# The same instructions on other SBUF addresses: new homes for the operands of TensorE

## The chip, the cores and the metric

The kernel runs on one NeuronCore of a Trainium2 chip. The metric is the device time of one execution in microseconds (us), the median of three runs. An address in this document is a byte offset within a partition of SBUF; "home" is the address at which a tile begins, and its remainder in 256 is what the change sets.

## The reference

Pooled attention, and then two products with a rational function between them:

```python
k_p = k.reshape(B, H, S // 8, 8, D).mean(axis=3)          # v_p the same
attn = softmax(q @ k_p.T / sqrt(D))                       # B = H = 8, S = 576, D = 64
x = (attn @ v_p).transpose(0, 2, 1, 3).reshape(4608, 512)
h = x @ w_in                                              # 512 x 2048
g = (a0 + a1*h + a2*h*h + a3*h**3) / (1 + |b0|*|h| + |b1|*h*h + 1e-6)
out = g @ w_out                                           # 2048 x 512
```

All inputs and the output are float32.

## The kernel before

The 4608 tokens are worked on in 18 blocks of 256, and the 2048 hidden columns in 8 units of 256. Every large operand is split into two parts, a rounded one and what is left of it (`x` into `xs[0]`, `xs[1]`; `w_in` into `win0` to `win7`; `w_out` into `wout0` to `wout7`; the rational's result into `gh`, `gl`), and a product is three passes over such parts. The parts are of the type float32r.

For block i and unit u, `mm1` makes `ph`: six groups of four matmuls. In each matmul a slice of 128x128 of `win{u}` is the stationary operand, which a LDWEIGHTS brings into the array, and 128x256 of x is the moving operand, which streams through. `rational` then makes `gh` and `gl` on ScalarE, VectorE and GpSimd, and `mm2` makes `po`: six groups of two matmuls, where 128x128 of `gh` or `gl` is stationary and 128x512 of `wout{u}` moves. The attention of a block (`ps`, `pm`, `pv` and so on) stands between such groups.

The order on every engine comes from a planner (`Plan.solve`), which lists all operations with estimated costs and due times and simulates the five engines; `Plan.issue` then issues them in that order. `mm2` of a unit is due four units after its `mm1` (`LAG`), so that TensorE goes back and forth: four matmuls of `mm1` of one unit, two of `mm2` of the unit four before, four of `mm1`, and so on. Such a piece of four and two is called a group here. In a steady stretch unit 1's groups hold products with `wout5`, unit 2's with `wout6` (the first still with `wout5`), and so on around. There are 18 x 8 x 6 = 864 pieces of each kind.

Tiles get their addresses from pools. A pool lays its tiles one behind the other in the order of their first use, in steps of 32 bytes, and the pools lie behind each other in the order in which they are opened. In the kernel before, all sixteen weight tiles stand in `cpool` together with small constants and the attention's tiles, `x` stands in `work2` behind the small tiles `mx` and `sm`, and `gh` and `gl` in `work3`. Every slice that a matmul reads begins a multiple of 256 bytes behind its tile's home (512 within `win`, 1024 within `x`, 2048 within `wout`, 512 or 1024 within `gh` and `gl`), and the buffers of a ring lie 2048 or 4096 bytes apart; so the remainder in 256 of a home holds for every slice of it.

Of the kernel before, what the change touches and what calls it, by code (L numbers as in the profile page):

```python
# [8 lines left out]
F32 = mybir.dt.float32  # L9
F32R = mybir.dt.float32r  # L10
# [62 lines left out]
class Buf:  # L73
# [7 lines left out]
    def real(self):  # L81
        if self.it is None:
            self.it = self.ring.pool.tile(self.shape, self.dtype, tag=self.ring.tag,
                                          name=self.name)
        return self.it
# [233 lines left out]
def tile_pooled_attention_then_rational_moe(  # L319
# [20 lines left out]
    P = 128  # L340
    G = 8
    SP = S // G
    NJ = H // 2
    REM = 2 * SP - P
    RW = G * D
    TOK = 256
# [10 lines left out]
    pools = {}  # L357

    def pool(name, bufs, loose=False, **kw):
        pools[name] = ctx.enter_context(tc.tile_pool(name=name, bufs=bufs, **kw)), bufs, loose  # L360

    pool("cpool", 1)
    pool("stage", 2)
    pool("work1", 1)
    pool("work2", 2)
    pool("dec", 2, loose=True)
    pool("rat", 5)
    pool("work3", 3)
    pool("ps", 8, loose=True, space=PS)
    pool("hbm", 1, space=bass.MemoryType.DRAM)  # L370

    def new(where, tag, shape, dtype, name):
        return plan.tile(*pools[where], shape, dtype, tag, name)

    def bank(name, shape):
        return new("ps", "ps", shape, F32, name)
# [5 lines left out]
    def pe(ns, calls, claims=(), after=()):  # L382
        return plan.add("pe", ns / 1000, calls, claims=claims, after=after)

    def mm(out, lhsT, rhs, start, stop):
        return "matmul", (out,), dict(lhsT=lhsT, rhs=rhs, start=start, stop=stop)

    def dma(kbytes, dst, src, run=2048, issue=0.48, early=60.0, after=()):

        plan.add("sp", issue, [("dma_start", (dst, src), {})], early=early, after=after,  # L390
                 bytes=kbytes * 1024 * (1 + 312 / run))
# [4 lines left out]
    real = pools["cpool"][0].tile  # L396
    ones = pools["dec"][0].tile([P, P], F32, tag="m", name="ones")
    identr = real([P, P], F32R, tag="identr", name="identr")
    ident = identr.bitcast(F32)
    zero = real([P, 1], F32R, tag="zero", name="zero")  # L400
    masks = new("cpool", "masks", [P, 6], F32, "masks")

    spread = new("work1", "vs", [P, 3 * P], F32, "fourfold")
# [4 lines left out]

    mrem_lo, mrem = ([masks[:, i + m:i + m + 1] for m in range(2)] for i in (2, 4))
    QC = 1.0 + 1e-6  # L410
    cbias = real([P, 1], F32, tag="cbias", name="cbias")

    def small(name, *args, **kw):
        plan.add("pool", 0.13, [(name, args, kw)])
# [30 lines left out]
    CW = 2 * DM  # L445
# [20 lines left out]
    spare = [["win7", "wout7", "wout6", "win6"], ["win5", "wout5", "wout4"]]  # L466
    held = {}

    def early(n, at):
        if (n, at) not in held:  # L470
            held[n, at] = new("cpool", spare[n][at], [P, 2 * CW], F32, f"early{n}_{at}")
        return held[n, at]

    w_in32, w_out32 = w_in.bitcast(I32), w_out.bitcast(I32)
# [1 line left out]

    def load_weights(kind, u):
        name = f"{kind}{u}"
        raw = new("cpool", name, [P, 2 * CW], F32, "r" + name)
        if kind == "win":  # L480
            dma(1024, raw.bitcast(I32).rearrange("p (k x) -> p k x", x=4 * P),
                w_in32[:, u * 4 * P:(u + 1) * 4 * P].rearrange("(k p) x -> p k x", p=P))
        else:
            dma(1024, raw.bitcast(I32).rearrange("p (f x) -> p f x", f=2),
                w_out32[u * 2 * P:(u + 1) * 2 * P, :].rearrange("(f p) x -> p f x", p=P), run=4096)
        words = raw.bitcast(I32).rearrange("p (n t) -> p n t", t=2)
        hw, lw = words[:, :, 1], words[:, :, 0]
        m = new("dec", "m", [P, CW], F32, f"m_{name}")
        mi = m.bitcast(I32)
        act(CW + 100).activation(m, hw.bitcast(F32), AF.Prelu, scale=2.0 ** -111, alpha=-2.0 ** 32)  # L490
        dve(CW, port=True, rate=0.52).tensor_scalar(
            out=mi, in0=mi, scalar1=3, scalar2=None, op0=ALU.logical_shift_left)
        dve(CW, port=True).scalar_tensor_tensor(
            out=mi, in0=lw, scalar=29, in1=mi, op0=ALU.logical_shift_right, op1=ALU.bitwise_or)
        w = new("cpool", name, [P, 2, CW], F32R, name)
        act(CW).copy(w[:, 0, :], m)
        gp(CW).tensor_tensor(out=w[:, 1, :], in0=m, in1=w[:, 0, :].bitcast(F32),
                             op=ALU.subtract)
        weights[kind, u] = w
# [165 lines left out]
    def segs(t0, n):  # L665

        r, t = [], t0
        while t < t0 + n:
            e = min(t0 + n, (t // S + 1) * S)
            r.append((t - t0, e - t0, t // S))  # L670
            t = e
        return r
# [148 lines left out]

    def values(i, hi, lo, before=None):

        xs = [new("work2", f"x{s}", [P, NJ, TOK], F32R, f"x{s}_{i}") for s in range(2)]
        for c in range(2):
            if before:
                before(c)
            pv = bank(f"pv{i}_{c}", [P, 2, TOK])
            calls = []
            for jj in range(2):  # L830
                j = 2 * c + jj
                for r0, r1, n in segs(i * TOK, TOK):
                    vh, vl = vm[n % 2]
                    o = pv[:, jj, r0:r1]
                    terms = ((o, vh[:, j, :], hi[:, j, r0:r1]), (o, vl[:, j, :], hi[:, j, r0:r1]),
                             (pv[:D, jj, r0:r1], vr[n % 2][:, j, :], lo[:, NJ + c, r0:r1]),
                             (o, vh[:, j, :], lo[:, j, r0:r1]))
                    calls += [mm(dst, vals, probs, s == 0, s == 3)
                              for s, (dst, vals, probs) in enumerate(terms)]
            pe(117.4 * 8 if len(calls) == 8 else 1635, calls, claims=xs)  # L840
            cs = slice(2 * c, 2 * c + 2)
            act(2 * TOK).copy(xs[0][:, cs, :], pv)
            dve(2 * TOK).tensor_tensor(
                out=xs[1][:, cs, :], in0=pv, in1=xs[0][:, cs, :].bitcast(F32),
                op=ALU.subtract)
        return xs
# [9 lines left out]
    def attend(i):  # L856
# [27 lines left out]
        if i >= SQ:  # L884

            for a in range(4):
# [15 lines left out]
            dve(2 * TOK, port=True).tensor_tensor(  # L902
                out=both[0], in0=both[1], in1=own, op=ALU.subtract)
        return values(i, hi, lo)


# [6 lines left out]
        return kept  # L913

    def reload(i, kept):
        xs = [new("work2", f"x{s}", [P, NJ, TOK], F32R, f"xr{s}_{i}") for s in range(2)]
        for x, d in zip(xs, kept):
            dma(512, x.bitcast(F32), d, run=4096)
        return xs
# [19 lines left out]

    def rational(i, u, ph):  # L940
        t, w, r = (new("rat", "rat", [P, 2, TOK], F32, f"{x}{i}_{u}") for x in "twr")
        gh = new("work3", "gh", [P, 2, TOK], F32R, f"gh{i}_{u}")
        gl = new("work3", "gl", [P, 2, TOK], F32R, f"gl{i}_{u}")
        rp = bank(f"rp{i}_{u}", [P, 2, TOK])

        n = 2 if last(i, u) else 1
        for k in range(n):
            f = slice(k, k + 1) if n == 2 else slice(0, 2)
            quotient(2 * TOK // n, *(x[:, f, :] for x in (ph, t, w, r, rp, gh, gl)),
                     (t, w, r), (gl,))  # L950
        return gh, gl

    def last(i, u):
        return i == NBLK - 1 and u == NU - 1

    def quotient(W, h, t, w, r, rp, gh, gl, early, late):
        act(W, claims=early).activation(w, h, AF.Abs, scale=1.0 / WS)
        act(W + 200).activation(t, h, AF.Identity, bias=na2, scale=na3)
        act(W + 260).activation(r, w, AF.Identity, bias=b0, scale=b1)
        gp(W).tensor_tensor(out=w, in0=w, in1=r, op=ALU.mult)  # L960
        dve(W).tensor_tensor(out=t, in0=t, in1=h, op=ALU.mult)
        dve(W + 50).scalar_tensor_tensor(
            out=t, in0=t, scalar=na1, in1=h, op0=ALU.add, op1=ALU.mult)
        act(W + 30).activation(rp, w, AF.Ln, bias=QC)
        act(W + 10).activation(rp, rp, AF.Exp, scale=-1.0)
        dve(W + 50).scalar_tensor_tensor(
            out=t, in0=t, scalar=na0, in1=rp, op0=ALU.add, op1=ALU.mult)
        dve(W).scalar_tensor_tensor(
            out=rp, in0=w, scalar=QC, in1=rp, op0=ALU.add, op1=ALU.mult)
        dve(W).scalar_tensor_tensor(  # L970
            out=t, in0=rp, scalar=-2.0, in1=t, op0=ALU.add, op1=ALU.mult)
        act(W, claims=late).copy(gh, t)
        gp(W).tensor_tensor(out=gl, in0=t, in1=gh.bitcast(F32), op=ALU.subtract)
# [73 lines left out]
    xs, kept = {}, {}  # L1047
    for at, (i, u) in enumerate(order):
# [19 lines left out]
        gh, gl = rational(i, u, ph)  # L1068
# [44 lines left out]
```

## Time and profile before

| | |
|---|---|
| median of 3 runs | 940.96 us (940.87 to 941.06) |
| profiled execution, first to last instruction | 940.1 us |
| TensorE matmul busy | 929.1 us, 99% |
| TensorE weight load busy | 845.3 us, 90% |
| VectorE, ScalarE, GpSimd busy | 763.6, 677.6, 530.8 us |
| `ph` matmuls, `po` matmuls | 3456 and 1728 |

The profile gives a span, from the first instruction to the last, and no other time of that execution; the 0.9 us between the span and the median lie around it. A matmul's busy time overlaps that of the next one, so what a matmul costs is read from the start of one to the start of the next, and not from its mean duration.

### The profile page before, as it was taken

Reading aid. Unit: us, or ns where it says so; the run is one execution under the profiler, and the core shown is the slowest. Engines: PE = TensorE matmul, PEld = TensorE weight load, DVE = VectorE, ACT = ScalarE, POOL = GpSimd, SP = SyncE. Lnnn points to the kernel's source line nnn. Section 1 sums busy time; section 2 is a strip of 40 time slices with the busy share of each in tenths; the row PEclk is TensorE's granted clock in tenths of the full one; section 3 lists DMA queues with packets and bytes.
Section 4 is the critical chain, followed back from the end, with each engine's and each line's share of the span. In section 5 each row is a group of like instructions: output and inputs, shape, how many; then the busy total and the mean of one; then the engine's idle time right before and its main releaser. Section 6 shows DMA issues by size and latency. Waiting matters only on the chain.

```text
span 940.1 us, 17117 instructions
## 1 busy us (share of the span) xinstructions
PE 929.1 (99%) x6158; PEld 845.3 (90%) x6158; DVE 763.6 (81%) x1335; ACT 677.6 (72%) x1126; POOL 530.8 (56%) x474
## 2 busy tenths in 40 slices
PE   7999999999999999999999999999999999999998
PEld 7899999989999999999999899999999899999996
DVE  6889987688879777878888788878886988787764
ACT  3788888667677767776776867686867786777764
POOL 5776788685447544445644574457543754444452
PEclk9999999999999999999999999999999999999999
DMA  9995201163233412122603160215212231202000
GB/s 282 306 378 176 46 29 46 40 161 87 47 79 76 115 24 58 26 59 51 141 9 70 41 155 10 39 41 129 69 27 53 68 80 23 57 1 58 1 23 23
DMA packets 185072, 75.32 MB, mean 80 GB/s; under 512 B 162332, under 2 KB 162332, under 8 KB 184988
## 3 DMA queue, kind: packets, MB, share of 16 engines
q1 hardware_dynamic: 184988, 74.23, 30.9%
q8 instruction: 49, 0.80, 0.4%
q14 instruction: 35, 0.29, 0.1%
HBM read 50.59 MB, written 12.58 MB: 67 GB/s over the span
## 4 chain that ended last, share of the span: by engine, by line
PE 95%; DMA 3%; SPq 2%; issue 0%; ACT 0%
PE po L299 43%; PE ph L299 43%; PE pv L299 4%; PE ps L299 4%; SPq L299 2%; DMA early<-in_v_dram 1%; DMA q<-in_q_dram 1%; PE pvs L299 1%; PE pk L299 0%; PE pvr L299 0%; PE pq L299 0%; PE pm L299 0%; PE po L290 0%; PE pr L299 0%; PE pl L299 0%
## 5 line engine op out<-in xcount | busy, mean ns | idle before, releaser
L299 PEld LDWEIGHTS ph<-x,win 128*128 128x128 f32 x3264 | 484.4, 188 | 61.7 <-DVE x L299 0.5
L299 PE MATMUL ph<-x,win 128*128 128x256 f32 x3264 | 507.5, 282 | 0.5 <-DVE x L299 0.3
L299 PE MATMUL po<-wout,gh 128*128 128x512 f32 x1152 | 356.9, 396 | 0.0
L299 POOL TENSOR_TENSOR w<-w,r 128x512 f32<-128x512 f32 (+1 forms) x145 | 193.8, 1336 | 269.9 <-ACT r L299 268.2
L299 POOL TENSOR_TENSOR gl<-t,gh 128x512 fp32r<-128x512 f32 (+1 forms) x145 | 190.8, 1316 | 79.5 <-ACT gh L299 78.2
L299 PEld LDWEIGHTS po<-wout,gh 128*128 128x128 f32 x1152 | 182.3, 189 | 7.8 <-issue 0.4
L299 PE MATMUL po<-wout,gl 128*128 128x512 f32 x576 | 181.7, 396 | 0.0
L299 DVE SCALAR_TENSOR_TENSOR t<-t,abn,rp 128x512 f32<-128x512 f32 (+1 forms) x145 | 106.9, 738 | 51.8 <-ACT rp L299 50.0
L299 ACT ACTIVATE t<-ph,abn 128x512 f32<-128x512 f32 (+1 forms) x145 | 112.2, 774 | 40.7 <-PE ph L299 30.2
L299 DVE TENSOR_TENSOR t<-t,ph 128x512 f32<-128x512 f32 (+1 forms) x145 | 97.8, 676 | 41.9 <-ACT t L299 41.0
L299 ACT ACTIVATE r<-w,abn 128x512 f32<-128x512 f32 (+1 forms) x145 | 117.7, 812 | 13.3 <-POOL gl L299 6.6
L299 ACT ACTIVATE w<-ph 128x512 f32<-128x512 f32 (+1 forms) x145 | 86.1, 594 | 54.8 <-PE ph L299 34.8
L299 ACT ACTIVATE rp<-w 128x512 f32<-128x512 f32 (+1 forms) x145 | 86.6, 597 | 41.8 <-POOL w L299 40.1
L299 ACT CAST gh<-t 128x512 fp32r<-128x512 f32 (+1 forms) x145 | 88.8, 613 | 37.7 <-DVE t L299 36.9
L299 DVE SCALAR_TENSOR_TENSOR t<-t,abn,ph 128x512 f32<-128x512 f32 (+1 forms) x145 | 106.4, 735 | 2.4
L299 DVE SCALAR_TENSOR_TENSOR t<-rp,t 128x512 f32<-128x512 f32 (+1 forms) x145 | 98.4, 679 | 2.4
L299 DVE SCALAR_TENSOR_TENSOR rp<-w,rp 128x512 f32<-128x512 f32 (+1 forms) x145 | 98.8, 681 | 0.3
L299 PEld LDWEIGHTS po<-wout,gl 128*128 128x128 f32 x576 | 89.5, 188 | 2.2 <-issue 0.2
L299 ACT ACTIVATE rp<-rp 128x512 f32<-128x512 f32 (+1 forms) x145 | 84.1, 580 | 2.6
L299 POOL TENSOR_TENSOR e<-e,sm 128x576 f32<-128x576 f32 x36 | 42.0, 1186 | 20.4 <-DVE sm L299 14.3
L299 PE MATMUL pv<-am,vm 128*128 128x256 f32 (+3 forms) x288 | 45.9, 279 | 0.0
L299 PEld LDWEIGHTS pv<-am,vm 128*128 128x128 f32 x288 | 41.9, 192 | 0.4
(109 smaller groups left out, 849.6 us busy)
## 6 DMA issues: line engine op xcount, KB each, us to landing
am<-e SPq DMA_DIRECT2D x224, 48.0 KB, 2.1
out_dram<-ob SPq DMA_DIRECT2D x17, 512.0 KB, 3.1
rwin<-in_moe_w_in_dram SPq DMA_DIRECT2D x8, 1024.0 KB, 10.1
rwout<-in_moe_w_out_dram SPq DMA_DIRECT2D x8, 1024.0 KB, 10.5
st_k<-in_k_dram SPq DMA_DIRECT2D x12, 512.0 KB, 4.7
st_v<-in_v_dram SPq DMA_DIRECT2D x12, 512.0 KB, 3.9
q<-in_q_dram SPq DMA_DIRECT2D x144, 32.0 KB, 1.9
st_v<-in_v_dram SPq DMA_DIRECT2D x48, 64.0 KB, 2.2
```

What stands on the lines that cost most here:

```text
L299: getattr(engines[op.eng], name)(*map(value, args), **{k: value(v) for k, v in kw.items()})
```

## The change

Tiles are spread over more pools, and the pools are opened in another order. `wout`, `xs` and `win` become pools of their own, in that order behind `cpool`; `consts` (two tiles of 32 bytes each, with `zero` and `cbias`) stands between `xs` and `win`; `gs` with the rational's halves `gh` and `gl` comes right behind `win`; `work2`, which now holds only `mx` and `sm`, goes to the end. No instruction is added, taken away or moved: on all five engines the programs have the same rows in the same order, with the same waits. Tiles of the first two batches' inputs (`early`) lie where the weights of a later unit will lie, as before, and so move with them.

The core of the diff:

```diff
     pool("cpool", 1)
+    pool("wout", 1)
+    pool("xs", 2)
+    pool("consts", 1)
+    pool("win", 1)
+    pool("gs", 3)
     pool("stage", 2)
     pool("work1", 1)
-    pool("work2", 2)
     pool("dec", 2, loose=True)
     pool("rat", 5)
-    pool("work3", 3)
+    pool("work2", 2)
...
-    zero = real([P, 1], F32R, tag="zero", name="zero")
+    zero = pools["consts"][0].tile([P, 1], F32R, tag="zero", name="zero")
...
-    cbias = real([P, 1], F32, tag="cbias", name="cbias")
+    cbias = pools["consts"][0].tile([P, 1], F32, tag="cbias", name="cbias")
...
-        raw = new("cpool", name, [P, 2 * CW], F32, "r" + name)
+        raw = new(kind, name, [P, 2 * CW], F32, "r" + name)
...
-        w = new("cpool", name, [P, 2, CW], F32R, name)
+        w = new(kind, name, [P, 2, CW], F32R, name)
...
-        xs = [new("work2", f"x{s}", [P, NJ, TOK], F32R, f"x{s}_{i}") for s in range(2)]
+        xs = [new("xs", f"x{s}", [P, NJ, TOK], F32R, f"x{s}_{i}") for s in range(2)]
...
-        gh = new("work3", "gh", [P, 2, TOK], F32R, f"gh{i}_{u}")
-        gl = new("work3", "gl", [P, 2, TOK], F32R, f"gl{i}_{u}")
+        gh = new("gs", "gh", [P, 2, TOK], F32R, f"gh{i}_{u}")
+        gl = new("gs", "gl", [P, 2, TOK], F32R, f"gl{i}_{u}")
```

The homes in the two built programs, each as its remainder in 256:

| tile | role in its matmul | before | after |
|---|---|---|---|
| `x` (all buffers) | moving, `mm1` | 192 | 0 |
| `win0`, `win1` | stationary, `mm1` | 0 | 64 |
| `win2`, `win3`, `win5` | stationary, `mm1` | 32 | 64 |
| `win4` | stationary, `mm1` | 64 | 64 |
| `win6`, `win7` | stationary, `mm1` | 192 | 64 |
| `gh`, `gl` (all buffers) | stationary, `mm2` | 192 | 64 |
| `wout0`, `1`, `2`, `4`, `5` | moving, `mm2` | 32 | 0 |
| `wout3` | moving, `mm2` | 64 | 0 |
| `wout6` | moving, `mm2` | 0 | 0 |
| `wout7` | moving, `mm2` | 224 | 0 |
| `am0`, `am1` (probabilities) | moving, `pv` | 64 | 64 |
| `vm` of even and odd batches | stationary, `pv` | 32, 64 | 224, 0 |

## Rows read from the trace of the kernel before

**Rows 1.** The page: busy time and share of each engine; the granted clock.

```profile
PE 929.1 (99%) x6158; PEld 845.3 (90%) x6158; DVE 763.6 (81%) x1335; ACT 677.6 (72%) x1126; POOL 530.8 (56%) x474
...
PEclk9999999999999999999999999999999999999999
```

**Rows 2.** The page: the chain that ended last, shares by engine.

```profile
PE 95%; DMA 3%; SPq 2%; issue 0%; ACT 0%
```

**Rows 3.** Waits of TensorE, the four longest: us in total, times, longest.

```profile
PE pq L299 <- DMA q<-in_q_dram: 2.9, 2, 2.6
PE idle L299 <- DVE identr L1076: 2.2, 1, 2.2
PE pvs L299 <- DMA early<-in_v_dram: 1.0, 1, 1.0
PE pr L299 <- ACT e L299: 0.5, 1, 0.5
```

**Rows 4.** TensorE's groups, shapes apart: count, busy us, mean ns.

```profile
L299 PE MATMUL ph<-x,win 128*128 128x256 f32 x3264 | 507.5, 282 | 0.5 <-DVE x L299 0.3 <-ACT x L299 0.2
L299 PE MATMUL po<-wout,gh 128*128 128x512 f32 x1152 | 356.9, 396 | 0.0
L299 PE MATMUL po<-wout,gl 128*128 128x512 f32 x576 | 181.7, 396 | 0.0
...
L299 PE MATMUL ph<-xr,win 128*128 128x256 f32 x192 | 29.3, 282 | 0.0
```

**Rows 5.** Timeline of TensorE, one group of block 11, unit 3: start, us.

```profile
603.47 0.63 PE L299 MATMUL ph<-x,win 128*128 128x256 f32 x4
603.94 0.63 PE L299 MATMUL po<-wout,gl 128*128 128x512 f32 x2
604.40 0.63 PE L299 MATMUL ph<-x,win 128*128 128x256 f32 x4
```

**Rows 6.** Timeline of the weight loads beside Rows 5: start, us.

```profile
603.83 0.30 PEld L299 LDWEIGHTS po<-wout,gl 128*128 128x128 f32 x2
604.18 0.65 PEld L299 LDWEIGHTS ph<-x,win 128*128 128x128 f32 x4
```

**Rows 7.** Timeline of TensorE, 584 to 627 us: ends of undisturbed runs of groups.

```profile
584.18 0.64 PE L299 MATMUL ph<-x,win 128*128 128x256 f32 x4
...
586.06 0.64 PE L299 MATMUL ph<-x,win 128*128 128x256 f32 x4
...
591.78 0.64 PE L299 MATMUL ph<-x,win 128*128 128x256 f32 x4
...
595.54 0.63 PE L299 MATMUL ph<-x,win 128*128 128x256 f32 x4
...
599.75 0.64 PE L299 MATMUL ph<-x,win 128*128 128x256 f32 x4
...
601.60 0.63 PE L299 MATMUL ph<-x,win 128*128 128x256 f32 x4
...
606.27 0.63 PE L299 MATMUL ph<-x,win 128*128 128x256 f32 x4
...
609.10 0.63 PE L299 MATMUL ph<-x,win 128*128 128x256 f32 x4
...
610.95 0.63 PE L299 MATMUL ph<-x,win 128*128 128x256 f32 x4
...
613.77 0.64 PE L299 MATMUL ph<-x,win 128*128 128x256 f32 x4
...
616.61 0.64 PE L299 MATMUL ph<-x,win 128*128 128x256 f32 x4
...
618.96 0.64 PE L299 MATMUL ph<-x,win 128*128 128x256 f32 x4
...
623.65 0.63 PE L299 MATMUL ph<-x,win 128*128 128x256 f32 x4
...
626.47 0.64 PE L299 MATMUL ph<-x,win 128*128 128x256 f32 x4
```

More of the change, by code (lines that the diff above doesn't have):

```diff
@@ L470, in early @@
         if (n, at) not in held:
-            held[n, at] = new("cpool", spare[n][at], [P, 2 * CW], F32, f"early{n}_{at}")
+            held[n, at] = new(spare[n][at][:-1], spare[n][at], [P, 2 * CW], F32, f"early{n}_{at}")
         return held[n, at]
@@ L915, in reload @@
     def reload(i, kept):
-        xs = [new("work2", f"x{s}", [P, NJ, TOK], F32R, f"xr{s}_{i}") for s in range(2)]
+        xs = [new("xs", f"x{s}", [P, NJ, TOK], F32R, f"xr{s}_{i}") for s in range(2)]
         for x, d in zip(xs, kept):
```

## The prediction, made before the changed kernel was run

> **What bounds the kernel now.** I read the page first. TensorE is busy 99% of the span at the full granted clock, and the weight load beside it 90%; the next engine, VectorE, has 81% [rows 1]. The chain that ended last runs over TensorE for 95% [rows 2], and of the 940.1 us it waited 2.9, 2.2 and 1.0 us, all for DMAs and the first constant of the start; the next wait of that view is 0.5 us [rows 3]. So the time is the sum of what the matmuls take one after the other, and a change that moves no instruction can act only through how fast a matmul follows the one before it. (The clock stands at 2.4 GHz, the higher of its two levels, in every slice of the page; nothing there moves.)
>
> The second view is the list of TensorE's groups: 3264 + 192 = 3456 matmuls of `ph` with 256 columns, and 1152 + 576 = 1728 of `po` with 512 [rows 4]. In fours and twos that is 864 groups. Their mean durations, 282 and 396 ns, overlap and say nothing of the pace.
>
> The third view is the timeline, and it gives the pace. One group runs from 603.47 to 604.40 us: 0.47 us for four `ph` and 0.46 for two `po`, some 118 and 230 ns a matmul [rows 5]. Beside it the timeline of the weight loads shows that the load for the next `ph` begins at 604.18 [rows 6], when the second `po` (half of the 0.46 behind 603.94, so 604.17) has just begun to stream. So at each moment two streams read SBUF in the same partitions: the moving operand of this matmul and the stationary operand of the next. What the change sets is how these two lie to each other. I write "a to b: d" for the remainder in 256 of the home of b less that of a, where a moves while b is loaded. There are four such pairs in a group: x to `win` (three times), x to `gh`/`gl`, `wout` to `gh`/`gl`, and `wout` to `win`.
>
> **What the homes are worth, from the trace of before.** The kernel before has its homes by accident, and they differ from unit to unit, so its own trace holds the experiment. I take runs of groups that no attention matmul breaks, and divide the time between the first and last start by the number of groups between [rows 7]. x to `gh`/`gl` is 0 in all of them.
>
> - Unit 0 (584.18 to 586.06, 2 groups): 940 ns. Unit 1 (591.78 to 595.54, 4): 940 ns. Both have x to `win` 64, `wout` to `g` 160, `wout` to `win` 224.
> - Unit 2 (599.75 to 601.60, 2): 925 ns, with 96, 192 and 32.
> - Unit 3 (601.60 to 606.27, 5): 934 ns, with 96, 224 and 64.
> - Unit 4 (609.10 to 610.95, 2): 925 ns, with 128, 160 and 32.
> - Unit 5 (613.77 to 616.61, 3): 947 ns, with 96, 160 and 0.
> - Unit 6 (618.96 to 623.65, 5): 938 ns, with 0, 160 and 160.
> - Unit 7 (623.65 to 626.47, 3): 940 ns, with 0, 128 and 128.
>
> Starts are given to 0.01 us, so a run of two groups is good to some 5 ns and a run of five to 2. The units' mean is 936 ns. The spread, 925 to 947, is far over that, and units 0 and 1, whose homes agree, agree too. The kernel runs the same kinds of matmul in all of them. I read it thus: a stationary operand that begins 32 or 64 bytes past the moving one gives the short groups (925, 925, 934), one that begins at the same remainder (0) or in the 32 bytes behind it (224 is 32 short of 256) gives the long ones (940, 940, 947, and 938 and 940 with x to `win` at 0).
>
> The Trainium skill speaks against such a reading: its page "TensorE: Matmul & The Clock Gate", section "Step-by-step: what each phase is for", says that TensorE has two independent read ports into SBUF and that loading the next weights takes no read bandwidth from the running matmul. By that rule homes can't matter, and the sum of this change would be nothing; the spread between units in the rows above disagrees with it, and I go by the rows, with the rule as a rival below.
>
> **The change part by part.** After it all four pairs stand at 64, in every unit, slice and buffer, since the slices lie multiples of 256 apart. What one group then takes is the one unknown.
>
> - `wout` to `win` 64: unit 3 has it (934), and 32 in units 2 and 4 (925). This is the pair that separates the units most.
> - x to `win` 64: units 0 and 1 have it, at 940 ns, but with `wout` to `win` at 224.
> - `wout` to `g` 64: no unit has it; unit 3, with 224, is the slowest of the three good ones.
> - x to `g` 64: no unit has it; it is 0 everywhere now, the value that goes with long groups in the other pairs.
>
> The mean of the three units with the stationary operand 32 or 64 past is 928 ns. Since two more pairs leave values that look bad or neutral, I take 927. The sum: (936 - 927) ns x 864 groups = 7.8 us off the profiled execution's 940.1 us, so 932.3, and with the 0.9 us that lie around the span 933.2 us.
>
> The bounds of that unknown: on the bad side the changed kernel could repeat in all units what unit 1 does (940, +3.5 us) or what unit 5 does (947, +9.5 us). On the good side, if x to `g` at 0 costs every unit now as much as lies between the mean and the best (936 - 925 = 11 ns), its removal beside the 925 gives 914 ns, 19.0 us less, 922.0 us.
>
> What else moves costs next to nothing. `pv`: its moving tiles keep 64, its stationary ones go to 224 and 0, so their pair goes from 224 and 0 to 160 and 192; by the same spread (22 ns in a group of six, 4 ns a matmul) some 300 such matmuls can move the sum by 1 us either way at the very most. The start: TensorE's waits there for q and v are 2.9 and 1.0 us in total [rows 3], a cap on what other DMA targets could give. The other engines read and write tiles on other addresses too, but TensorE's longest wait for one of them behind the start is 0.5 us [rows 3], so a few ns on an instruction there stay hidden; they would have to make TensorE wait to cost anything, and VectorE with 19% of its time free [rows 1] leaves room for groups that are 1% shorter.
>
> **The rivals.**
>
> 1. A better lock than any now: all four pairs at once give 914 to 923 ns. 922 to 929.8 us. For it: no unit now has all pairs past each other. Against it: the two best units, with different x to `win` (96 and 128), stop at the same 925, which looks like a floor.
> 2. Nothing measurable: what decides isn't the remainder but what went before (how the matmul falls on the stream of the load), the new homes give one pace for all units and it is about today's mean, 934 to 938 ns, so 939 to 942.7 us. For it: the two best runs here are only two groups long. Against it: units 0 and 1 agree. By the rule of the Trainium skill's page "TensorE: Matmul & The Clock Gate" named above, this would be the outcome as well.
> 3. Slower, by one mechanism: the pair that occurs three times in a group, x to `win`, is what sets the pace, and at 64 it is unit 1's. Then all 864 groups run at unit 1's 940 ns, 3.5 us more: 944.4 us. It decides from a group of 938.2 ns upwards (1.9 us over 864 groups is 2.2 ns over 936). Against it: units 2 and 3 share x to `win` and differ by 9 ns, units 6 and 5 show that neither pair alone explains the order.
>
> A difference of under 0.2%, 1.9 us, is about what a measurement of this kernel can't tell from no change.
>
> **How the numbers follow.** My forecast, a group of 924 to 933 ns and so 930.6 to 938.4 us, has a chance of 0.52. Rival 1 has 0.14, rival 2 has 0.18, rival 3 (up to unit 5's 947) 0.16. Faster by over 0.2%, below 939.1 us, are the forecast and rival 1 and a little of rival 2's edge: 0.67. Within 0.2%: 0.17. Slower: 0.16. The range reaches into both neighbours: 926 us leaves out the far end of rival 1, and 943.5, just under unit 1's price, the far end of rival 3. The likeliest case's own range is the 930.6 to 938.4 above.
>
> **What would show each step.** In the profile after, the same timeline should show groups of about 0.93 us in every unit, with no unit apart from the others: unit 5's three groups, 2.84 us now, should take about 2.78, and unit 1's four, 3.76 now, about 3.71. If the units still differ by 20 ns, the remainder in 256 isn't what decides. If they agree at 0.94 or more, rival 3 is right, and x to `win` decides. TensorE's waits should stay near 7 us in total; if they grow by microseconds, another engine has become slower on its new addresses, which nothing here lets me expect. The prediction is wrong above all if the pace depends on address bits above the lowest eight, since these change for every tile and I have given them no price.

## The result, and the profile after

The changed kernel takes 927.78 us (927.0 to 928.65, 4 runs) against 941.01 us (940.87 to 942.29, 4 runs): a ratio of 0.9859, 95% interval 0.9845 to 0.9873, so 13.2 us or 1.4% faster. That is inside the range (926.0 to 943.5) near its low end, and 5.4 us below the 933.2 that was forecast. It is the time of the first rival, a better lock than any before, at 922 to 929.8 us.

The page of the profile after: the span, the busy time of each engine, the granted clock, and the widest row of TensorE's matmuls.

```profile
span 926.9 us, 17117 instructions
PE 916.0 (99%) x6158; PEld 834.1 (90%) x6158; DVE 764.6 (82%) x1335; ACT 677.1 (73%) x1126; POOL 529.7 (57%) x474
...
PEclk9999999999999999999999999999999999999999
...
L299 PE MATMUL ph<-x,win 128*128 128x256 f32 x3264 | 497.5, 279 | 0.8 <-ACT x L299 0.5
```

The other engines' busy times are those of before to within 1.1 us [rows 1], at the same clock; TensorE's alone fell, its matmuls' by 13.1 us and its weight loads' by 11.2. The mean duration of a `ph` matmul fell from 282 ns [rows 4] to 279 only, which shows once more that this column says little of the pace.

Waits of TensorE after: us in total, times, longest.

```profile
PE pq L299 <- DMA q<-in_q_dram: 3.4, 2, 3.0
PE idle L299 <- DVE identr L1080: 2.2, 1, 2.2
PE pr L299 <- ACT e L299: 0.5, 1, 0.5
```

These are the waits of before [rows 3], less the 1.0 us for v at the start and with 0.5 us more for q. So nothing new is waited for, and nothing that was waited for explains 13 us.

The timeline of TensorE after, for five of the units of [rows 7]: first and last start of runs of groups that no attention matmul breaks.

```profile
576.25 0.62 PE L299 MATMUL ph<-x,win 128*128 128x256 f32 x4
...
578.09 0.62 PE L299 MATMUL ph<-x,win 128*128 128x256 f32 x4
...
584.71 0.62 PE L299 MATMUL ph<-x,win 128*128 128x256 f32 x4
...
587.47 0.62 PE L299 MATMUL ph<-x,win 128*128 128x256 f32 x4
...
593.45 0.62 PE L299 MATMUL ph<-x,win 128*128 128x256 f32 x4
593.91 0.62 PE L299 MATMUL po<-wout,gh 128*128 128x512 f32 x2
594.37 0.62 PE L299 MATMUL ph<-x,win 128*128 128x256 f32 x4
...
598.05 0.62 PE L299 MATMUL ph<-x,win 128*128 128x256 f32 x4
...
598.97 1.53 PE L299 MATMUL ph<-x,win 128*128 128x256 f32 x12
600.34 0.62 PE L299 MATMUL po<-wout,gh 128*128 128x512 f32 x2
...
605.40 0.62 PE L299 MATMUL ph<-x,win 128*128 128x256 f32 x4
...
608.16 0.62 PE L299 MATMUL ph<-x,win 128*128 128x256 f32 x4
...
610.47 0.62 PE L299 MATMUL ph<-x,win 128*128 128x256 f32 x4
...
615.07 0.62 PE L299 MATMUL ph<-x,win 128*128 128x256 f32 x4
```

Unit 0: 1.84 us for two groups. Unit 1: 2.76 for three. Unit 3: 4.60 for five. Unit 5: 2.76 for three. Unit 6: 4.60 for five. All are 920 ns, where before they were 940, 940, 934, 947 and 938 [rows 7]. Of the 609 groups of the whole execution that stand free (no attention matmul in them, and under 980 ns from start to start), 558 take 920 ns and 26 take 915; the mean is 920.3, and before it was 937.2.

One more stretch isolates the narrow matmuls: when unit 4 begins, twelve `ph` follow each other. They take 600.34 - 598.97 = 1.37 us, 114 ns each. In the kernel before the same twelve took 1.42 us, 119 each:

```profile
607.21 1.59 PE L299 MATMUL ph<-x,win 128*128 128x256 f32 x12
608.63 0.62 PE L299 MATMUL po<-wout,gh 128*128 128x512 f32 x2
```

### The profile page after: what moved, and what is told of

Its sections match the earlier page's. It is cut to its first block, busy times and chain, and to the rows that moved or that the text cites. A ratio compares the mean times of both kernels' runs of the same rounds, so it can differ in the third digit from the quotient of the medians.

```text
span 926.9 us, 17117 instructions
## 1 busy us (share of the span) xinstructions
PE 916.0 (99%) x6158; PEld 834.1 (90%) x6158; DVE 764.6 (82%) x1335; ACT 677.1 (73%) x1126; POOL 529.7 (57%) x474
## 4 chain that ended last, share of the span: by engine, by line
PE 92%; DVE 2%; SPq 2%; ACT 1%; DMA 1%; issue 0%; POOL 0%; ACTq 0%
PE po L299 41%; PE ph L299 41%; PE pv L299 4%; PE ps L299 4%; SPq L299 2%; DMA q<-in_q_dram 1%; DVE t L299 1%; PE pvs L299 0%; PE pq L299 0%; DVE e L299 0%; DVE sm L299 0%; PE pk L299 0%; DVE am L299 0%; PE pm L299 0%; PE pvr L299 0%
## 5 line engine op out<-in xcount | busy, mean ns | idle before, releaser
L299 PE MATMUL ph<-x,win 128*128 128x256 f32 x3264 | 497.5, 279 | 0.8 <-ACT x L299 0.5
L299 PEld LDWEIGHTS po<-wout,gh 128*128 128x128 f32 x1152 | 179.7, 188 | 7.7 <-issue 0.4
```

The lines of the kernel that those rows point to most:

```text
L299: getattr(engines[op.eng], name)(*map(value, args), **{k: value(v) for k, v in kw.items()})
```

## The experiments

All change homes alone: a constant's tile is made wider, or pools are opened in another order, and the instructions stay as they are. All twelve were run beside the kernel before, each on one chip with it; nine have one time each and a profile, the three with more say so. The kernel before itself took 940.1 to 942.7 us in the 15 runs beside e64, so a single time is good to 2 or 3 us. Steadier yardsticks are the mean spacing of the free groups, worked out as above from the starts, and the twelve `ph` in a row (median of the 14 such stretches). "d" is the home of the loaded operand less that of the moving one, in 256.

| run | x to win | x to g | wout to g | wout to win | us | ns a free group | twelve `ph`, ns |
|---|---|---|---|---|---|---|---|
| before | by unit | 0 | by unit | by unit | 941.0 | 937.2 | 1425 |
| changed | 64 | 64 | 64 | 64 | 927.8 | 920.3 | 1365 |
| off0 | 0 | 0 | 0 | 0 | 936.9 | 934.8 | 1432 |
| off32 | 32 | 32 | 32 | 32 | 943.0 | 941.2 | 1434 |
| abs32 | 64 | 64 | 64 | 64 | 928.0 | 920.4 | 1365 |
| off96 | 96 | 96 | 96 | 96 | 942.8 | 939.4 | 1422 |
| off128 | 128 | 128 | 128 | 128 | 943.0 | 941.2 | 1421 |
| off192 | 192 | 192 | 192 | 192 | 940.4 | 938.4 | 1413 |
| off320 | 64 (+256) | 64 (+256) | 64 (+256) | 64 (+256) | 927.4 | 920.4 | 1365 |
| g0 | 64 | 0 | 0 | 64 | 933.0 | 928.0 | 1365 |
| win0 | 0 | 64 | 64 | 0 | 934.8 | 928.5 | 1415 |
| e128 | 64 | 192 | 64 | 192 | 932.1 | 926.3 | 1412 |
| e192 | 64 | 128 | 64 | 0 | 933.3 | 929.8 | 1374 |
| e64 | 64 | 0 | 64 | 128 | 939.9 | 938.4 | 1376 |

**The difference, or the address itself.** abs32 moves all four homes 32 bytes up and keeps the differences; the other three keep the moving homes at 0 and move the loaded ones, through the width of `zero` in `consts`.

```diff
 abs32
-    bands = new("cpool", "bands", [P, 4], F32, "bands")
+    bands = new("cpool", "bands", [P, 12], F32, "bands")
 off0 (49), off128 (17), off192 (33), off32 (57), off96 (9), off320 (65)
-    zero = pools["consts"][0].tile([P, 1], F32R, tag="zero", name="zero")
+    zero = pools["consts"][0].tile([P, 49], F32R, tag="zero", name="zero")[:, 0:1]
```

Expected of abs32: 

> All four homes 32 bytes further than in the changed kernel: moving ones at 32, loaded ones at 96, the difference still 64. Theory A: 920 ns a group and 928 us, as the changed kernel. Theory B: the multiple of 64 is lost, so a pace like that of the kernel before, 930 to 945 ns and 936 to 948 us. Theory C: as A.

Expected of off0: 

> All four homes (x, input weights, output weights, rational's halves) at 0 in 256, so that the loaded operand begins at the same remainder as the moving one in all pairs. Theory A, the difference of the two homes in 256 sets the pace: 0 went with the long groups before, so 940 ns a group or more and 944 to 952 us. Theory B, it is enough that every home is a multiple of 64: a group stays at 920 ns, 928 us. Theory C, the pattern repeats in 128 bytes: slow as in A, and then equal to the run at 128.

Expected of off128: 

> Moving homes at 0, loaded ones at 128 in 256. Theory A: no group before had 128 in all pairs; unit 4 had it for x and its weights in its groups of 925 ns, so 920 to 930 ns and 928 to 936 us. Theory B: 920 ns, 928 us. Theory C: the same pace as with all homes at 0, 940 ns or more.

Expected of off192: 

> Moving homes at 0, loaded ones at 192 in 256, that is 64 short of the moving one's next 256. Theory A: like the 224 of units 0 and 1 before, 935 to 942 ns and 940 to 946 us. Theory B: 920 ns, 928 us. Theory C: the same as the changed kernel's 64, 920 ns and 928 us.

Measured: 928.01, 936.91, 943.01 and 940.35 us, with the kernel before at 940.26. The timeline of abs32:

```profile
600.40 0.62 PE L299 MATMUL ph<-x,win 128*128 128x256 f32 x4
...
604.08 0.62 PE L299 MATMUL ph<-x,win 128*128 128x256 f32 x4
```

Four groups in 3.68 us: 920 ns, as in the changed kernel, though every home now is 32 past a multiple of 64. Theory B, that a multiple of 64 does it, falls twice: abs32 lost nothing, and off0, off128 and off192, whose homes are all multiples of 64, lost the gain. Theory C, a pattern of 128 bytes, falls with off192, which should have equalled the changed kernel. Theory A holds in kind and misses in size: I had expected off128 at 928 to 936 us, and it is slower than the kernel before, while off0 is not the worst case but one of the better ones.

The timeline of off0 shows how its mean comes about:

```profile
606.34 0.64 PE L299 MATMUL ph<-x,win 128*128 128x256 f32 x4
...
607.28 0.63 PE L299 MATMUL ph<-x,win 128*128 128x256 f32 x4
...
608.20 0.64 PE L299 MATMUL ph<-x,win 128*128 128x256 f32 x4
...
609.15 0.63 PE L299 MATMUL ph<-x,win 128*128 128x256 f32 x4
...
610.07 0.64 PE L299 MATMUL ph<-x,win 128*128 128x256 f32 x4
```

Starts 0.94, 0.92, 0.95 and 0.92 us apart, on one set of homes: the kernel goes back and forth between two main paces (255 of its 609 free groups take 925 ns, 264 take 941 or 942). They take turns. Of the 209 groups of 925 ns that another free group follows, all are followed by one of 938 or more, and of 222 groups of 941 or 942, 221 are followed by one of 925. And one and the same place of a block, the last products with `wout5` beside unit 2's first matmuls, takes 925 ns in eight of the 14 blocks where it stands free, and 941 or 942 in the other six. So at equal homes the pace of a group goes with what ran before it. off192 shows a like thing, right behind the twelve `ph`:

```profile
606.00 1.58 PE L299 MATMUL ph<-x,win 128*128 128x256 f32 x12
607.41 0.62 PE L299 MATMUL po<-wout,gh 128*128 128x512 f32 x2
607.87 0.62 PE L299 MATMUL ph<-x,win 128*128 128x256 f32 x4
608.33 0.62 PE L299 MATMUL po<-wout,gh 128*128 128x512 f32 x2
608.78 0.63 PE L299 MATMUL ph<-x,win 128*128 128x256 f32 x4
...
609.72 0.63 PE L299 MATMUL ph<-x,win 128*128 128x256 f32 x4
```

The first free group takes 0.91 us, the fastest group seen in any run (25 of its 609 take 907 to 909, eight of them right behind the twelve), and the next is back at 0.94, where 538 of them lie. In four other blocks the group at the same place takes 0.94 us at once.

**How narrow the good distance is.**

Expected of off32: 

> Moving homes at 0, loaded ones at 32. If any small step past the moving home does (theory A as read from the kernel before, where 32 from output to input weights stood in the two best units): one pace for all units, 915 to 930 ns, 924 to 936 us. If 64 is a special distance (theory D: the good distance is narrow): two or more paces as with all homes at 0, mean 930 ns or more, 936 us or more.

Expected of off96: 

> Moving homes at 0, loaded ones at 96. Theory A with a window that begins past 0 and ends before 128: 915 to 925 ns and 924 to 932 us. Theory D, 64 alone is good: 930 ns or more and 936 us or more, as at 128.

Measured: 942.95 and 942.81 us, with the kernel before at 940.45. Theory D is right, and the reading of the prediction, that 32 or 64 past is good, is wrong in its first half: 32 in all pairs is as slow as 96 and 128. Among the six distances that were tried, 64 stands alone; 160 and 224 in all pairs were not tried.

Expected of off320: 

> The changed kernel with 256 bytes more between the moving and the loaded homes: 320 for 64, the remainder in 256 stays 64. If the remainder in 256 is what counts: 920 ns a group, 928 us. If the pattern is longer (512 or more, which no kernel so far could tell, since slices step by 512): 930 ns or more, 936 us or more.

Measured: 927.38 us, 920.4 ns, 1365 ns. A further 256 bytes change nothing, so the remainder in 256 is what counts.

**Which pairs.** g0 takes the halves alone to 0, win0 the input weights alone, by a constant's tile of the right width between the two pools.

```diff
 g0 (48, bands 12), win0 (16, bands 12, and zero 49)
+    pool("padb", 1)
     pool("gs", 3)
...
-    abn = new("cpool", "abn", [P, 8], F32, "abn")
+    abn = new("padb", "abn", [P, 48], F32, "abn")
```

Expected of g0: 

> The changed kernel with the rational's halves alone at 0: x to input weights and output weights to input weights stay 64, x to halves and output weights to halves become 0. If the pair that counts is the one with the input weights (theory P1): 920 ns, 928 us. If all pairs have to stand at 64 (theory P2): 930 ns or more, 936 us or more, mostly lost in the two wide matmuls.

Expected of win0: 

> The changed kernel with the input weights alone at 0: x to halves and output weights to halves stay 64, x to input weights and output weights to input weights become 0. Theory P1, the input weights' pairs count: as with all homes at 0 or worse, 934 ns and 937 us or more. If the halves' pairs count (theory P3): near 920 ns and 928 us. Theory P2, all pairs are needed: 930 ns or more.

Measured: 932.98 and 934.82 us. Each lost 8 ns of the 17 that separate the changed kernel from the one before, g0 in its wide matmuls, win0 in both. The timeline of g0:

```profile
601.74 1.53 PE L299 MATMUL ph<-x,win 128*128 128x256 f32 x12
603.10 0.63 PE L299 MATMUL po<-wout,gh 128*128 128x512 f32 x2
...
605.42 0.62 PE L299 MATMUL ph<-x,win 128*128 128x256 f32 x4
605.88 0.63 PE L299 MATMUL po<-wout,gh 128*128 128x512 f32 x2
606.35 0.62 PE L299 MATMUL ph<-x,win 128*128 128x256 f32 x4
...
610.98 0.62 PE L299 MATMUL ph<-x,win 128*128 128x256 f32 x4
```

Six groups from 605.42 to 610.98 are 5.56 us, 927 ns; the twelve `ph` take 1.36, as after; the four `ph` of a group 0.46, as after; and the two `po` 0.47 for 0.46. g0 moves two pairs at once, x to `g` and `wout` to `g`; by where the time fell, x to `g` at 0 cost nothing here, and `wout` to `g` at 0 cost the 7 or 8 ns. P1 and P3 fall. P2 (all pairs are needed) is nearest, though both runs came in under its bound of 930 ns, at 928.0 and 928.5. With win0 the twelve `ph` went to 1415 ns, the pace of other distances, so x to `win` away from 64 loses that stretch. But x to `win` at 64 alone doesn't keep it, as e128 below shows.

**The last pair.** e128, e192 and e64 keep both x to `win` and `wout` to `g` at 64 and move x and `win` together against `wout` and `g`, which changes the two pairs that cross.

```diff
     pool("wout", 1)
-    pool("xs", 2)
     pool("consts", 1)
-    pool("win", 1)
     pool("gs", 3)
+    pool("padb", 1)
+    pool("xs", 2)
+    pool("padc", 1)
+    pool("win", 1)
```

(e64 has no `padb`. The two pads hold small constants whose widths set the distances, and the width of `bands` keeps `wout` at 0.)

Expected of e128: 

> x and the input weights together 128 further than the output weights and the halves, by another order of the pools: x to input weights 64, output weights to halves 64, x to halves 192, output weights to input weights 192 (64 in the changed kernel). If only the pairs x to input weights and output weights to halves have a price (theory P4): 920 ns, 928 us. If the pair from output weights to input weights counts too: it loses, 924 to 935 ns and 931 to 941 us, or gains, as 908 ns groups did at 192, 910 ns and 919 us.

Expected of e192: 

> As the run before with 192 for 128: x to input weights 64, output weights to halves 64, x to halves 128, output weights to input weights 0. Theory P4: 920 ns, 928 us. If the pair from output weights to input weights has a price of its own, its value 0 should lose: part of the 7 ns that the run with the input weights alone at 0 lost, up to 927 ns and 934 us.

Expected of e64: 

> x and the input weights together 64 further than in the changed kernel, beside the output weights and the halves: x to input weights 64, output weights to halves 64, x to halves 0, output weights to input weights 128. The run with the halves alone at 0 had x to halves at 0 and kept its four narrow matmuls as they were, so that pair should be free. Theory P4, the other two pairs alone count: 920 ns a group, 928 us. Theory P6, all of the loads behind the wide matmuls count, output weights to input weights too: 926 to 930 ns, 932 to 936 us, as at 192 and 0. A gain on the changed kernel, 910 to 915 ns and 919 to 924 us, if 64 is no more than one of several values for that pair and 128 suits the two slow spacings (236 and 118 ns) better.

Measured: e128 932.06 us (4 runs; ratio to before 0.991, 0.9893 to 0.9926), e192 933.33 (4 runs; 0.9924, 0.9909 to 0.9939), e64 939.90 (11 runs; 0.999, 0.9981 to 0.9999). None beats the changed kernel. P4, that the crossing pairs are free, falls in all three. In time, e128 and e192 lie where the theories of a price for `wout` to `win` had them (e192's 929.8 ns a group is 3 ns over); but x to `g` moved with that pair in both, so the times don't say which of the two has the price. For e64 I had 932 to 936 us at the most, and it gave up nearly all of the gain. Its timeline:

```profile
600.03 0.64 PE L299 MATMUL ph<-x,win 128*128 128x256 f32 x4
...
600.98 0.63 PE L299 MATMUL ph<-x,win 128*128 128x256 f32 x4
...
601.91 0.64 PE L299 MATMUL ph<-x,win 128*128 128x256 f32 x4
...
602.86 0.63 PE L299 MATMUL ph<-x,win 128*128 128x256 f32 x4
...
606.62 1.54 PE L299 MATMUL ph<-x,win 128*128 128x256 f32 x12
608.00 0.63 PE L299 MATMUL po<-wout,gh 128*128 128x512 f32 x2
```

The groups go 0.95, 0.93, 0.95 us, while the twelve `ph`, where but for the ends only x and `win` meet, still take 1.38 us. So here the narrow matmuls by themselves keep their gain, and the alternation with the wide ones undoes it. e128 has x to `win` at 64 too, and there the twelve lost theirs:

```profile
600.66 1.57 PE L299 MATMUL ph<-x,win 128*128 128x256 f32 x12
602.08 0.63 PE L299 MATMUL po<-wout,gh 128*128 128x512 f32 x2
```

They take 1.42 us, as in the kernel before. So the stretch isn't set by x to `win` alone either.

**Where in a group the time lies.** The starts of the single matmuls give six spacings a group. The table has their means over the 609 free groups, in ns; the second row names the pair that acts in each, the operand that moves and the one that is loaded meanwhile for the next matmul.

| run | `ph` 1 to 2, 2 to 3, 3 to 4 | `ph` 4 to `po` 1 | `po` 1 to 2 | `po` 2 to next `ph` |
|---|---|---|---|---|
| pair | x to `win` | x to `g` | `wout` to `g` | `wout` to `win` |
| before | 118, 118, 118 | 118 | 233 | 232 |
| changed | 118, 114, 113 | 113 | 226 | 236 |
| g0 | 118, 114, 114 | 114 | 233 | 236 |
| win0 | 116, 113, 117 | 117 | 230 | 236 |
| e128 | 117, 117, 118 | 119 | 229 | 226 |
| e192 | 118, 116, 115 | 118 | 229 | 233 |
| e64 | 120, 120, 116 | 116 | 234 | 233 |

Two things stand out. The changed kernel's last spacing, where `wout` to `win` is at 64, is no better than before: it takes 236 ns, as with that pair at 0 in win0, and 226 with it at 192 in e128. So 64 isn't shown to be a good distance for that pair by itself. And a price doesn't stay in the spacing of its pair: e64 has `wout` to `g` at 64 and takes 234 ns there against 226, and e128 and e64 have x to `win` at 64 and lose 3 to 6 ns in its second and third spacing. So the set as a whole sets the pace, and no single pair's price is shown. The e runs also move x against `wout`, and so one moving operand against the other; a price of that can't be told from these runs apart from the crossing pairs.

## Why the prediction came out as it did

**What bounds the kernel: right.** TensorE at 99%, no wait that matters, and the whole gain in the spacing of its matmuls. 13.2 us came off the span (940.1 to 926.9). From start to start, the `ph` matmuls gained 10.3 us of them, the `po` 2.1 and `pv` 0.9; the rest cancels to 0.1. The 609 free groups make 10.3 us (937.2 to 920.3 ns each), and the other 255, most of them broken by attention matmuls, only 2.1. So the narrow matmuls, in which x moves, gained most, and not the spacing of `wout` to `win`, the pair that the prediction had as separating the units most.

**The homes work through their difference: right, and now shown**, by abs32 and off320 against off0 and off192. The kernel before was a weaker experiment on itself than the prediction took it for: that homes matter could be seen in it, but which distance is good could not, since a unit has several paces at the same homes. Unit 2's first free groups with `wout6` take 0.94 and 0.93 us:

```profile
596.47 0.64 PE L299 MATMUL ph<-x,win 128*128 128x256 f32 x4
...
597.41 0.63 PE L299 MATMUL ph<-x,win 128*128 128x256 f32 x4
...
598.34 0.64 PE L299 MATMUL ph<-x,win 128*128 128x256 f32 x4
```

To the ns they are 940 and 925, and the two of [rows 7] are 930 and 926; the prediction's 925 for unit 2 had taken those two alone.

**The rule of two ports: the rows disagree with it.** The Trainium skill's page "TensorE: Matmul & The Clock Gate", section "Step-by-step: what each phase is for", has the next weights' load take no read bandwidth from the running matmul. The runs disagree: the changed kernel and off128, with the same matmuls in the same order at the same granted clock (0.998), stand at 920 and 941 ns a group, with the moving homes at 0 in both and the loaded ones at 64 and 128. The other tiles that this shifts are no way out, since abs32 and off320 shift them too, by 32 and 256 bytes, and lose nothing. The measurement decides. What in SBUF or in the engine makes them meet isn't shown by these runs.

**The step that failed: the size of the one unknown.** The prediction put a group at 927 ns, from the mean of the three units "with the stationary operand 32 or 64 past" and the hope that two more pairs leave bad values; it measured 920.3. Those 6.7 ns over 864 groups are 5.8 us, about the 5.4 by which the forecast missed. The reasoning under it was worse than its result: off32 shows that 32 is no good distance, so the 32 of units 2 and 4 doesn't explain their 925. Their groups stand right behind breaks in the order (two products in a row, the twelve `ph`), and may be moments of a kernel that, like off0, moves between paces; that isn't shown. The 925 that "looks like a floor", the argument against the first rival, was no floor. That rival's 914 to 923 ns holds what came. That the time came inside the range owes something to luck: a reading that took 32 and 64 as alike met a change that sets all pairs to 64, and with 32 in all pairs the kernel takes 943 us (off32).

**The slower rival, that x to `win` alone sets the pace: wrong.** x to `win` is 64 in units 0 and 1 before (940), in e64 (938) and in the changed kernel (920).

**The rival by which nothing measurable comes: wrong in its outcome, and half right in its mechanism.** The changed kernel is 13.2 us faster and its free groups keep one pace, so homes do decide there. But what went before does set the pace of a group in off0, at one set of homes.

**Spread over units: right.** The prediction asked for one pace in all units, 2.78 us for three groups of unit 5; they take 2.76. **The small terms: right.** At the start the wait for q grew by 0.5 us and the one for v, 1.0 us, is gone, and `pv` gained 0.9 us where 1 was the most allowed.

**Open:** why 64 is the distance, which of the pairs have to have it, and what decides which pace a kernel with other distances falls into. Distances that aren't multiples of 32, 160 and 224 in all pairs, and the two crossing pairs one at a time weren't tried.

## What to carry to other kernels

When TensorE streams without a gap and its matmuls still take a per cent or two longer in one place than in another, compare the places' operand addresses: here the same instructions ran from 920 to 941 ns a group by the homes alone, and the starts in a timeline show it to a few nanoseconds where mean durations don't. Put operands into pools by their role (moving or loaded), so that one difference holds for all of them; a layout in order of first use gives each tile its own remainder. Don't expect to find the good distance by adding prices of single pairs: try the whole set, in steps of 32 bytes over 256, each with one profile.

## What was not expected of the hardware

One set of homes can have several paces, and groups take them in turn: 925 and 941 or 942 ns in off0, 946 or 947 and then 933, 934 or 929 in e64. A group of 908 ns exists (off192, 25 of 609), 12 ns under the changed kernel's 920, but no home that was tried holds it. And the same distance in all four pairs isn't better than none, unless it is 64: off32, off96 and off128 (943.0, 942.8 and 943.0 us) are all slower than off0 at 936.9.
